# Decoding float64 weights on chip: the sign through a Prelu scaling, two bit operations in place of three, the weights of w2 in SBUF

## The chip, the cores and the metric

The kernel runs on one core of a Trainium2 chip. The metric is the device time of one execution in microseconds: 1180.98 us, the median of three runs (1179.63, 1183.80 and 1180.98 us). The engines of the core are TensorE (PE, matmuls, with its weight loads shown as PEld), VectorE (DVE), ScalarE (ACT), GpSimd (POOL) and SyncE (SP, which issues all DMAs here). Each works through its own instructions in order and waits on semaphores for the others.

## The reference

Three layers on 4608 tokens of width 512. Chunked attention: eight batches, eight heads, chunks of 64 tokens; then a SiLU layer of width 2048; then a layer of width 1024 with a softmax-weighted gate and a normalisation:

```
scores = scale * q_c @ k_c.T ; attn = softmax(scores) ; x = attn @ v_c
h = x @ w_in ;  x2 = (h * sigmoid(h)) @ w_out
h = x2 @ w_in2 ; solu = h * softmax(h)
ln = (solu - mean) / sqrt(var + 1e-6) * g_ln ;  out = ln @ w_out2
```

The four weight matrices arrive as float64 (w1 = w_in, w2 = w_out, w3 and w4 those of the last layer); q, k and v are float32.

## The kernel before

The tokens go through in nine blocks of 512. Every matrix product is made of three fp16 products: each operand is kept as a high and a low half (`split`, L107: the high half by ACT with a scale, the low half by a subtraction on DVE or POOL), and high x high, high x low and low x high are summed in PSUM. Blocks 0 and 1 multiply in this plain way (`h_group`, L357; `x_part`, L637). From block 2 on the layers use seven block products in place of eight (`h_fast`, `x_fast`, `m_fast`), whose weight sums are formed once, during blocks 1 and 2 (`w1_sums`, `w2_sums`, `w3_sums`), written to DRAM and streamed back through a ring of buffers.

A float64 weight has no engine type, so it is loaded as pairs of 32-bit words and decoded on chip, 128x512 values (a tile) at a time: 48 tiles, namely 16 of w1, 16 of w2 (index 16 to 31), 8 of w3 and 8 of w4. A tile goes through three steps, called in a software pipeline (`d1`, `d2`, `d3`, L869 to L887):

- `dec_scale` (L124): ACT reads the high word as if it were a float32 and multiplies it by a power of two, which moves the exponent into place.
- `dec_bits` (L131): DVE shifts the result left by three (L136), ORs in the top three bits of the low word (L137), and ORs in the sign bit, which the shift has lost, from the high word (L139). The scaled words p lie in PSUM for the tiles below `SB` = 32 (tile `wp`), from there on in SBUF (tile `wy`).
- `dec_split` (L142): the two halves, high on ACT (L110), low on POOL (L114), for w4 low on DVE (L115), with the factor g_ln folded in.

Where the decode calls stand among the other work is fixed by lists: `START` for the first 30 us or so (block 0's attention), `NW0` and `NX` during block 0, `NW1` and `NX1` during block 1; a scheduler then puts each engine's instructions in order, with the decode at a lower priority in places (`high_priority(offset=-50)`). The weight loads (`fetch`, L852) go through four SBUF buffers, and a tile's load is issued once an earlier tile's bits are done. `ytile` (L861) names the SBUF buffers for decoded tiles: five in turn up to tile 27, two from 28 on.

Attention of the next block runs inside the second layer of the present one (`step`, L977): scores, softmax, split of the softmax in a_norm (L229; the low half, L237, on POOL for block 0's calls, else on DVE), a DMA transpose (pT), and the product with v (a_pv, L256 to L258), which also needs v's halves vbh (ACT) and vbl (DVE). The second layer's chain of normalisation is `m_norm` (L740): row maximum (L670), exponential (L764), product (L766), and so on, while the scores h_ps stay in PSUM.

Of the kernel before, what the change touches and what calls it, by code (L numbers as in the profile page):

```python
# [40 lines left out]
S_LN = 2.0 ** 10  # L41

LEAST = -3.4028234663852886e38


@with_exitstack
def fused(ctx: ExitStack, tc: tile.TileContext, qkv, w1, w2, w3, w4, g_ln, out):
# [22 lines left out]
    QF = 14  # L70
    DEFER = 7

    const = ctx.enter_context(tc.tile_pool(name="const", bufs=1))
# [24 lines left out]
    mhalf = const.tile([P, 1], F32, name="mhalf")  # L98
    zero = const.tile([P, 1], F32, name="zero")


# [22 lines left out]
    def dec_scale(c):  # L124
        st, y, wh, wl, gain = c
        if c[1] is None:
            c[1] = ps1.tile([P, 512], I32, tag="mm", name="wp")
        p = c[1]
        A.activation(p.bitcast(F32), st[:, :, 1].bitcast(F32), AF.Copy, scale=2.0 ** -111)

    def dec_bits(c, y):  # L131
        st, p, wh, wl, gain = c
        c[1] = y
        if y is None:
            c[1] = y = p
        V.tensor_scalar(out=p, in0=p, scalar1=3, scalar2=None, op0=ALU.logical_shift_left)  # L136
        V.scalar_tensor_tensor(out=p, in0=st[:, :, 0], scalar=29, in1=p,  # L137
                               op0=ALU.logical_shift_right, op1=ALU.bitwise_or)
        V.scalar_tensor_tensor(out=y, in0=st[:, :, 1], scalar=-2 ** 31, in1=p,  # L139
                               op0=ALU.bitwise_and, op1=ALU.bitwise_or)  # L140

    def dec_split(c):  # L142
        st, y, wh, wl, gain = c
        yf = y.bitcast(F32)
        if len(wh.shape) == 3:
            yf = yf.rearrange("p (a b) -> p a b", a=wh.shape[1])
        if gain is None:
            split(wh, wl, yf, 1.0, A, G)
        else:
            split(wh, wl, yf, gain, A, V)  # L150

# [679 lines left out]
    G.memset(mhalf, -0.5)  # L831
    G.memset(zero, 0.0)
    ident = one.tile([P, P], F32, tag="h2", name="ident")
    make_identity(nc, ident)
# [24 lines left out]

    SB = 32  # L860
    def ytile(i):  # L861
# [22 lines left out]
    def d3():  # L884
        if out_:
            i, c = out_.pop(0)
            dec_split(c)  # L887

# [6 lines left out]
    for x in FIRST:  # L895
# [6 lines left out]
        else:  # L902
            t = len(vs0)
            vs0.append(one.tile([P, 512], F32, tag=("vs", "xb0", "xb1", "xb2")[t], name=f"vs0_{t}"))
            nc.sync.dma_start(out=vs0[t], in_=qkv[t, :, 2])
    nc.sync.dma_start(out=gs, in_=g_ln)


# [21 lines left out]
    for b in range(NB):  # L930
# [46 lines left out]
        def step(s):  # L977
# [13 lines left out]
            if s in AT_S:  # L991
# [3 lines left out]
                if i < 3:  # L995
                    prep_qk(m + ORDER[i + 1], V if b == 1 else G)
                a_norm(n, eng_l=V if b else G)
            if s in AT_P:
# [74 lines left out]
```

## Time and profile before

| | |
|---|---|
| median of three runs | 1180.98 us |
| the profiled execution, first to last instruction | 1179.4 us |
| TensorE busy | 1127.8 us, 96% |
| VectorE busy | 911.7 us, 77% |
| ScalarE busy | 802.8 us, 68% |
| GpSimd busy | 249.1 us, 21% |
| DMA, mean over the span | 177 GB/s |

The profile is of one execution, whose span of 1179.4 us lies close to the fastest of the runs. A busy share is an average over stages: the decode fills the first 190 us, and there the engines are used differently from the rest. In the rows below an instruction is named by its line, its engine, and the tile that it writes and reads (out<-in). A duration given for one instruction can overlap its neighbour's by a little, since an engine starts the next one before the last has drained. "Idle before" is the time in which the engine stood still ahead of such instructions, with what released it.

### The profile page before, as it was taken

The numbers are of one execution on the slowest core, as the hardware profiler recorded it, in microseconds if no ns is written. First come the engines' busy times: TensorE is split into PE (matmuls) and PEld (weight loads), VectorE is DVE, ScalarE is ACT, GpSimd is POOL, SyncE is SP. The second block draws the span as 40 slices with busy tenths as digits, with TensorE's granted clock in tenths as the row PEclk, the third lists the DMA queues.
The fourth block names the chain that finished last, engine by engine and source line by source line (L and its number), as shares of the span: only waits on it lengthen the run. The fifth ranks groups of instructions, "written<-read, shape, count | busy, mean of one in ns | idle before, by whom it ended". The sixth has DMA issues, their size and how long they took to land.

```text
span 1179.4 us, 23566 instructions
## 1 busy us (share of the span) xinstructions
PE 1127.8 (96%) x9036; PEld 769.1 (65%) x9036; DVE 911.7 (77%) x1638; ACT 802.8 (68%) x1475; POOL 249.1 (21%) x243
## 2 busy tenths in 40 slices
PE   5999998998999999999999999999999999999998
PEld 4444443444657875887678767876787677777853
DVE  5999998487578787888778877888689868886453
ACT  6886678676667777856785677568756876577253
POOL 3655433334101510021003100310031002100001
PEclk9999899999999999999999999999999999999999
DMA  7667488543536564776577657666776676665704
GB/s 259 225 190 206 155 233 268 165 135 112 139 113 203 165 189 133 204 204 202 143 192 213 196 151 188 204 198 155 182 211 198 161 180 197 179 161 137 210 21 116
DMA packets 205169, 209.18 MB, mean 177 GB/s; under 512 B 120192, under 2 KB 130432, under 8 KB 205056
## 3 DMA queue, kind: packets, MB, share of 16 engines
q1 hardware_dynamic: 205056, 207.68, 61.5%
q8 instruction: 70, 1.15, 0.4%
q14 instruction: 43, 0.35, 0.1%
HBM read 156.24 MB, written 24.12 MB: 153 GB/s over the span
## 4 chain that ended last, share of the span: by engine, by line
PE 59%; DVE 16%; ACT 10%; DMA 7%; issue 6%; POOL 2%; SPq 0%; ACTq 0%; POOLq 0%; DVEq 0%
PE o_ps L821 5%; PE o_ps L813 5%; PE o_ps L814 5%; PE pa L491 3%; PE pa L594 3%; PE pa L592 3%; PE pa L593 3%; PE pa L493 3%; PE pa L492 3%; DVE vbl L115 2%; PE pa L708 2%; PE pa L709 2%; PE pa L710 2%; PE pb L491 2%; PE pb L493 2%
## 5 line engine op out<-in xcount | busy, mean ns | idle before, releaser
L110 ACT ACTIVATE q<-hc 128x512 f16<-128x512 f32 x196 | 119.1, 624 | 41.4 <-DVE hc L579 16.4
L115 DVE SCALAR_TENSOR_TENSOR q<-hc,q 128x512 f16<-128x512 f32 x196 | 138.0, 719 | 6.9 <-ACT q L110 5.5
L114 POOL TENSOR_TENSOR qbl<-qk,qbh 64x512 f16<-64x512 f32 x54 | 71.0, 1314 | 266.2 <-ACT qbh L110 223.6
L593 PE MATMUL pa<-q,ring 128*128 128x256 f16 x448 | 122.1, 273 | 0.0
L592 PE MATMUL pa<-q,ring 128*128 128x256 f16 x448 | 122.1, 273 | 0.0
L594 PE MATMUL pa<-q,ring 128*128 128x256 f16 x448 | 122.1, 273 | 0.0
L813 PE MATMUL o_ps<-w4h,uT 128*128 128x512 f16 x288 | 109.1, 379 | 0.4 <-DVE e L766 0.4
L814 PE MATMUL o_ps<-w4l,uT 128*128 128x512 f16 x288 | 109.2, 379 | 0.0
L779 POOL TENSOR_TENSOR c<-c,mhalf 128x2 f32<-128x2 f32 (+1 forms) x22 | 14.1, 640 | 392.1 <-DVE c L778 382.2
L492 PEld LDWEIGHTS <-ring 128*128 128x128 f16 x784 | 77.0, 98 | 18.4 <-issue 7.9
L491 PEld LDWEIGHTS <-ring 128*128 128x128 f16 x784 | 77.0, 98 | 11.5 <-DMA ring<-w1s 0.8
L592 PEld LDWEIGHTS <-ring 128*128 128x128 f16 x784 | 76.7, 98 | 11.1
L593 PEld LDWEIGHTS <-ring 128*128 128x128 f16 x784 | 76.7, 98 | 11.0
L493 PEld LDWEIGHTS <-ring 128*128 128x128 f16 x784 | 77.0, 98 | 9.2
L594 PEld LDWEIGHTS <-ring 128*128 128x128 f16 x784 | 76.7, 98 | 8.9
L821 PE MATMUL o_ps<-w4h,uT 128*128 128x512 f16 x288 | 70.2, 379 | 0.0
L491 PE MATMUL pa<-x,ring 128*128 128x256 f16 x224 | 61.6, 275 | 6.7 <-ACT hc L513 4.3
L493 PE MATMUL pa<-x,ring 128*128 128x256 f16 x224 | 61.7, 275 | 0.0
L492 PE MATMUL pa<-x,ring 128*128 128x256 f16 x224 | 61.6, 275 | 0.0
L491 PE MATMUL pb<-x,ring 128*128 128x256 f16 x224 | 61.1, 273 | 0.6 <-DMA ring<-w1s 0.6
L592 PE MATMUL pb<-q,ring 128*128 128x256 f16 x224 | 61.1, 273 | 0.0
L593 PE MATMUL pb<-q,ring 128*128 128x256 f16 x224 | 61.1, 273 | 0.0
(277 smaller groups left out, 3486.4 us busy)
## 6 DMA issues: line engine op xcount, KB each, us to landing
ring<-w1s SPq DMA_DIRECT2D x196, 256.0 KB, 3.4
ring<-w2s SPq DMA_DIRECT2D x196, 256.0 KB, 3.8
wst<-w SPq DMA_DIRECT2D x48, 512.0 KB, 4.1
qk<-qkv SPq DMA_DIRECT2D x29, 512.0 KB, 3.8
vs<-qkv SPq DMA_DIRECT2D x36, 256.0 KB, 3.2
out<-o SPq DMA_DIRECT2D x36, 256.0 KB, 2.2
w1s<-ws SPq DMA_DIRECT2D x32, 128.0 KB, 2.1
w2s<-ws SPq DMA_DIRECT2D x16, 256.0 KB, 2.0
```

Of the source, the lines that this page charges most:

```text
L110: A.activation(dst_h, src, AF.Copy, scale=scale)
L114: return G.tensor_tensor(out=dst_l, in0=src, in1=dst_h, op=ALU.subtract).ins
L115: return V.scalar_tensor_tensor(out=dst_l, in0=src, scalar=scale, in1=dst_h, op0=ALU.mult, op1=ALU.subtract).ins
L491: T.matmul(ps[:, c], wh, x[:, 0, k], start=first, stop=False, skip_group_check=True)
L492: T.matmul(ps[:, c], wh, x[:, 1, k], start=False, stop=False, skip_group_check=True)
L493: T.matmul(ps[:, c], wl, x[:, 0, k], start=False, stop=k == 1, skip_group_check=True)
L592: T.matmul(ps[:, c], wh, g[:, 0], start=first, stop=False, skip_group_check=True)
L593: T.matmul(ps[:, c], wh, g[:, 1], start=False, stop=False, skip_group_check=True)
L594: T.matmul(ps[:, c], wl, g[:, 0], start=False, stop=q == 1 and f == 3, skip_group_check=True)
L813: T.matmul(ps, uh[:, k], w4h[:, k, :], start=k == 0, stop=False)
L814: T.matmul(ps, uh[:, k], w4l[:, k, :], start=False, stop=False)
L821: T.matmul(ps, ul[:, k], w4h[:, k, :], start=False, stop=k == K2 - 1)
```

## The change

The scaling becomes a Prelu with a scale of 2^-108 and a slope of -2^32 for negative input. A negative value comes out positive, with an exponent 32 higher; the shift by three then moves that 32 into the sign bit. So the sign is there after the shift, and the third bit operation falls away. All values are now too large by 2^24, and `dec_split` brings them back by `S_D` = 2^-24: for even tiles (V) the factor stands in both halves' operations, and the low half moves from POOL to DVE; for odd tiles of w1 (G) POOL multiplies the value in place by a constant tile `down` and subtracts; for odd tiles from w2 on (A) ACT scales the value in place, and POOL subtracts. For w4 the factor goes into gs, once, on POOL. `SB` goes from 32 to 16, so that w2's tiles lie in SBUF from the scaling on. The softmax's low half (L237) is on DVE in every block.

```diff
@@ constants
+S_D = 2.0 ** -24
+    WAYS = "VG" * 8 + "VA" * 12
+    down = const.tile([P, 1], F32, name="down")
@@ dec_scale
-        A.activation(p.bitcast(F32), st[:, :, 1].bitcast(F32), AF.Copy, scale=2.0 ** -111)
+        A.activation(p.bitcast(F32), st[:, :, 1].bitcast(F32), AF.Prelu, scale=2.0 ** -108, alpha=-2.0 ** 32)
@@ dec_bits
         V.tensor_scalar(out=p, in0=p, scalar1=3, scalar2=None, op0=ALU.logical_shift_left)
-        V.scalar_tensor_tensor(out=p, in0=st[:, :, 0], scalar=29, in1=p,
+        V.scalar_tensor_tensor(out=y, in0=st[:, :, 0], scalar=29, in1=p,
                                op0=ALU.logical_shift_right, op1=ALU.bitwise_or)
-        V.scalar_tensor_tensor(out=y, in0=st[:, :, 1], scalar=-2 ** 31, in1=p,
-                               op0=ALU.bitwise_and, op1=ALU.bitwise_or)
@@ dec_split
-        if gain is None:
-            split(wh, wl, yf, 1.0, A, G)
-        else:
-            split(wh, wl, yf, gain, A, V)
+        if gain is not None:
+            return split(wh, wl, yf, gain, A, V)
+        way = WAYS[i]
+        if way == "A":
+            A.activation(yf, yf, AF.Copy, scale=S_D)
+            return split(wh, wl, yf, 1.0, A, G)
+        if way == "G":
+            A.activation(wh, yf, AF.Copy, scale=S_D)
+            G.tensor_tensor(out=yf, in0=yf, in1=down.to_broadcast([P, 512]).rearrange("p (a b) -> p a b", a=KD)
+                            if len(yf.shape) == 3 else down.to_broadcast([P, 512]), op=ALU.mult)
+            return G.tensor_tensor(out=wl, in0=yf, in1=wh, op=ALU.subtract)
+        split(wh, wl, yf, S_D, A, V)
@@ further down
+    G.memset(down, S_D)
-    SB = 32
+    SB = 16
-            dec_split(c)
+            dec_split(c, i)
+    G.tensor_scalar(out=gs, in0=gs, scalar1=S_D, scalar2=None, op0=ALU.mult)
-                a_norm(n, eng_l=V if b else G)
+                a_norm(n)
```

The scheduler's order changes on DVE, ACT, POOL and SP; on PE it is the same. DVE has 1491 listed rows in place of 1519, POOL 137 in place of 140 and ACT 1125 in place of 1121. The listing numbers lines by each version's own file, so that the bits' L137 is L141 afterwards, and `split`'s low half L115 is L119.

First, DVE at the first normalisation of the last layer, during block 1; mp is the row maximum of the scores h_ps, e the product with the exponential. Before:

```order
L670 TENSOR_REDUCE mp<-h_ps 128x1 x2
L115 SCALAR_TENSOR_TENSOR w4l<-wy,gs,w4h 128x512
L672 TENSOR_REDUCE mm__1781<-mp 128x1
L137 SCALAR_TENSOR_TENSOR wy<-wst,wy 128x512
L761 TENSOR_SCALAR nm<-mm__1781 128x1
L136 TENSOR_SCALAR wy<-wy 128x512
L139 SCALAR_TENSOR_TENSOR wy<-wst,wy 128x512
L137 SCALAR_TENSOR_TENSOR wy<-wst,wy 128x512
L139 SCALAR_TENSOR_TENSOR wy<-wst,wy 128x512
L766 SCALAR_TENSOR_TENSOR e,us<-h_ps,u 128x512
```

The same place afterwards, with the last of the decode ahead of it:

```order
L141 SCALAR_TENSOR_TENSOR wy<-wst,wy 128x512
L119 SCALAR_TENSOR_TENSOR w4l<-wy,gs,w4h 128x512
L680 TENSOR_REDUCE mp<-h_ps 128x1 x2
L682 TENSOR_REDUCE mm__1745<-mp 128x1
L771 TENSOR_SCALAR nm<-mm__1745 128x1
L776 SCALAR_TENSOR_TENSOR e,us<-h_ps,u 128x512
```

The last tiles' bits stand ahead of the maximum now, not between it and the product.

Second, DVE in the first 30 us; am is the row maximum of a softmax of block 0, ae its exponentials, w_0 the first tile of w1. Before:

```order
L271 TENSOR_REDUCE am<-s_ps 128x8
L139 SCALAR_TENSOR_TENSOR wy<-wst,wp 128x512
L280 TENSOR_SCALAR am<-am 128x8
L286 TENSOR_SCALAR as<-as 128x8
L288 RECIPROCAL ar<-as 128x8
L271 TENSOR_REDUCE am<-s_ps 128x8
L290 TENSOR_TENSOR ae_225<-ae_225,ar 128x512
L280 TENSOR_SCALAR am<-am 128x8
L136 TENSOR_SCALAR wp<-wp 128x512
```

The same place afterwards:

```order
L281 TENSOR_REDUCE am<-s_ps 128x8
L119 SCALAR_TENSOR_TENSOR w_0_72<-wy,w_0_72 128x512
L290 TENSOR_SCALAR am<-am 128x8
L296 TENSOR_SCALAR as<-as 128x8
L298 RECIPROCAL ar<-as 128x8
L300 TENSOR_TENSOR ae_228<-ae_228,ar 128x512
L281 TENSOR_REDUCE am<-s_ps 128x8
L140 TENSOR_SCALAR wp<-wp 128x512
L290 TENSOR_SCALAR am<-am 128x8
```

The fourth softmax's maximum (the second am here) has moved behind the third's normalisation, and a shift stands between it and its scaling.

Third, POOL before, where it splits the first softmax for block 1 (ae), among the halves of q, k and w2:

```order
L114 TENSOR_TENSOR w2t<-wy,w2t 128x512 x3
L114 TENSOR_TENSOR qb<-qk,qb 64x8x64
L237 TENSOR_TENSOR ae<-ae 128x512
L114 TENSOR_TENSOR qb<-qk,qb 64x8x64
L114 TENSOR_TENSOR w2t<-wy,w2t 128x512 x2
```

And DVE afterwards, where that split stands now:

```order
L244 TENSOR_TENSOR ae<-ae,ar 128x512
L225 TENSOR_REDUCE am<-s_ps 128x8
L119 SCALAR_TENSOR_TENSOR w2t<-wy,w2t 128x512
L247 TENSOR_TENSOR ae<-ae 128x512
L230 TENSOR_SCALAR am<-am 128x8
```

The split (L237, now L247) left POOL's queue and stands on DVE, two rows behind the normalisation that it needs.

## Rows read from the trace of the kernel before

**Rows 1.** The page: busy us and share of each engine; granted clock in 40 slices.

```profile
PE 1127.8 (96%) x9036; PEld 769.1 (65%) x9036; DVE 911.7 (77%) x1638; ACT 802.8 (68%) x1475; POOL 249.1 (21%) x243
...
PEclk9999899999999999999999999999999999999999
```

**Rows 2.** Stretches: from:to, length, busy us of PE, PEld, DVE, ACT, POOL; PEclk, DMA.

```profile
30.00:70.00 40.00, 39.86 (x180) 17.78 (x179) 36.34 (x59) 34.63 (x63) 22.95 (x20) 0.96 0.65 217
70.00:120.00 50.00, 46.24 (x350) 23.07 (x348) 45.96 (x79) 37.15 (x89) 28.75 (x26) 0.97 0.67 200
120.00:150.00 30.00, 27.80 (x140) 13.21 (x141) 28.64 (x38) 21.29 (x36) 11.45 (x9) 0.89 0.49 144
150.00:200.00 50.00, 43.51 (x213) 20.70 (x212) 46.66 (x101) 40.25 (x74) 19.41 (x21) 1.00 0.88 263
320.00:1179.40 859.40, 844.30 (x7166) 621.26 (x7164) 659.46 (x1182) 571.58 (x981) 116.09 (x108) 1.00 0.62 173
90.00:100.00 10.00, 7.92 (x71) 4.05 (x70) 9.09 (x15) 6.89 (x13) 8.34 (x8) 0.83 0.84 220
120.00:130.00 10.00, 7.80 (x43) 3.78 (x44) 9.14 (x13) 6.63 (x12) 4.35 (x4) 0.66 0.57 184
```

**Rows 3.** PE's waits, 50 to 150, then 150 to 200: us, times, longest.

```profile
PE x_ps L256 <- ACT vbh L110: 2.1, 1, 2.1
PE x_ps L256 <- DMA pT<-ae: 2.1, 1, 2.1
PE x_ps L258 <- DVE vbl L115: 0.9, 2, 0.6
...
PE wq L391 <- DVE e L766: 2.9, 1, 2.9
PE h_ps L362 <- DVE y L406: 2.1, 1, 2.1
PE h_ps L362 <- ACT g L366: 0.8, 1, 0.8
```

**Rows 4.** DVE's groups, 20 to 200: xcount, busy us, mean ns, idle before.

```profile
L137 DVE SCALAR_TENSOR_TENSOR wp<-wst,wp 128x512 int32<-128x512 int32 x31 | 21.0, 687 | 0.2
L136 DVE TENSOR_SCALAR wp<-wp 128x512 int32<-128x512 int32 x31 | 21.0, 692 | 1.5 <-ACT wp L129 1.5
L139 DVE SCALAR_TENSOR_TENSOR wy<-wst,wp 128x512 int32<-128x512 int32 x31 | 20.8, 680 | 1.4 <-POOL w2t L114 1.0
L139 DVE SCALAR_TENSOR_TENSOR wy<-wst,wy 128x512 int32<-128x512 int32 x16 | 14.5, 904 | 0.3
L137 DVE SCALAR_TENSOR_TENSOR wy<-wst,wy 128x512 int32<-128x512 int32 x16 | 14.1, 878 | 0.3
L115 DVE SCALAR_TENSOR_TENSOR w4l<-wy,gs,w4h 128x512 f16<-128x512 f32 x8 | 7.4, 933 | 0.0
L136 DVE TENSOR_SCALAR wy<-wy 128x512 int32<-128x512 int32 x16 | 7.2, 449 | 0.4 <-ACT wy L129 0.4
```

**Rows 5.** Groups of ACT and POOL, 20 to 200 us, same columns.

```profile
L129 ACT ACTIVATE wy<-wst 128x512 f32<-128x512 f32 x16 | 10.8, 677 | 11.3 <-POOL w3q L114 6.7 <-DVE w4l L115 3.1 <-POOL w2t L114 1.4
...
L114 POOL TENSOR_TENSOR w2t<-wy,w2t 128x512 f16<-128x512 f32 x16 | 19.4, 1215 | 17.5 <-ACT w2t L110 12.1 <-DMA vs<-qkv 5.4
L237 POOL TENSOR_TENSOR ae<-ae 128x512 f16<-128x512 f32 x4 | 4.6, 1156 | 5.2 <-issue 5.2
```

**Rows 6.** Timeline of ACT at 28.9 us: start, us, instruction.

```profile
28.87 0.57 ACT L110 ACTIVATE x<-x_ps 128x512 f16<-128x512 f32 x1
```

**Rows 7.** Timeline of four instructions; in brackets the idle time before and its releaser.

```profile
86.16 0.61 ACT L236 ACTIVATE ae<-ae 128x512 f16<-128x512 f32 x1
...
88.04 1.15 POOL L237 TENSOR_TENSOR ae<-ae 128x512 f16<-128x512 f32 x1
...
118.57 0.69 DVE L139 SCALAR_TENSOR_TENSOR wy<-wst,wp 128x512 int32<-128x512 int32 x1 [1.05 <-POOL w2t L114]
...
119.29 0.63 ACT L110 ACTIVATE w2t<-wy 128x512 f16<-128x512 f32 x1 [2.46 <-DVE wy L139]
```

More of the change, by code (lines that the diff above doesn't have):

```diff
@@ L136, in dec_bits, with dec_split @@
         V.tensor_scalar(out=p, in0=p, scalar1=3, scalar2=None, op0=ALU.logical_shift_left)
-        V.scalar_tensor_tensor(out=p, in0=st[:, :, 0], scalar=29, in1=p,
+        V.scalar_tensor_tensor(out=y, in0=st[:, :, 0], scalar=29, in1=p,
                                op0=ALU.logical_shift_right, op1=ALU.bitwise_or)
-        V.scalar_tensor_tensor(out=y, in0=st[:, :, 1], scalar=-2 ** 31, in1=p,
-                               op0=ALU.bitwise_and, op1=ALU.bitwise_or)
-    def dec_split(c):
+    def dec_split(c, i):
         st, y, wh, wl, gain = c
```

## The prediction, made before the changed kernel ran

> **What bounds the kernel now.** I read the busy shares and the granted clock first [rows 1]: TensorE (PE) is busy 96% of 1179.4 us at a clock that is full in nearly every slice, so what is left to win is PE's idle time and its half-clock stretches. The stretches say where these are [rows 2]. From 320 us to the end PE is busy 844.30 of 859.4 us, and no weight is decoded there. From 70 to 200 us, the stretch of the decode that the change touches, PE loses 3.76 + 2.20 + 6.49 = 12.45 us, and the clock falls to 0.83 in 90 to 100 us and to 0.66 in 120 to 130 us: 10 x 0.17 = 1.7 us and 10 x 0.34 = 3.4 us of matmul time on top, each behind a wait of PE. VectorE (DVE) is busy 92 to 95% there, ScalarE (ACT) 71 to 81%, GpSimd (POOL) 38 to 58%. In 30 to 70 us DVE is nearly as full (91%), but PE stands still for 0.14 us only, so a faster decode buys nothing there.
>
> PE's waits [rows 3] name the two kinds of loss. In 50 to 150 us it waits 2.1 us for pT, the transposed softmax, 2.1 us for vbh and 0.9 us for vbl; in 150 to 200 us 2.9 + 2.1 us for e and y from DVE and 0.8 us for g from ACT. No wait is on a weight as such: PE waits for attention and normalisation steps that stand behind decode work on the in-order engines. Sum of these waits: 10.9 us; with the clock, 16.0 us. That is about the most a lighter decode can give back.
>
> **The change, part by part.** Durations are the means of [rows 4, 5].
>
> *w1, 16 tiles, bits still in PSUM.* Before 692 + 687 + 680 ns, after 692 + 687: 16 x 0.68 = 10.9 us less on DVE. Half of the tiles (V) now subtract on DVE: no row has this subtraction, it reads two SBUF operands. Between 0.69 (bits on PSUM) and 0.93 (w4l, the nearest form) I take 0.88, the bits on SBUF: 8 x 0.88 = 7.0. Net -3.9 us, beside a PE that doesn't wait in 30 to 70 us: nothing on the path.
>
> *w2, 16 tiles, bits moved to SBUF.* Before 16 x 2.06 = 32.9 us. After, shift 0.449 and or 0.878: 16 x 1.33 = 21.2, and 8 V subtractions 7.0: 28.3. Net -4.7 us.
>
> *w3, 8 tiles.* Before 8 x (0.449 + 0.878 + 0.904) = 17.8; after 8 x 1.33 + 4 x 0.88 = 14.1. Net -3.7 us.
>
> *w4, 8 tiles.* One operation of 0.904 less each: -7.2 us.
>
> *Block 1's attention split.* L237 goes from POOL (four of 1.156 us) to DVE: 4 x 0.88 = +3.5 us.
>
> DVE in sum: -3.9 - 4.7 - 3.7 - 7.2 + 3.5 = -16.0 us, of 157.6 us that it is busy in 30 to 200 us [rows 2]. POOL loses 40 subtractions and L237 and gains 8 multiplications and 20 subtractions, 16 x 1.2 = 19 us less. ACT gains 12 scalings of 0.68 (its SBUF to SBUF copy) = +8.1 us in 70 to 150 us, where it is busy 58.4 of 80 us: it becomes 83% full, still not the bound. Prelu has no row; I put it at the copy it replaces, bounded by 48 x 0.05 = 2.4 us either way (ACT's copies of this size differ by that: 0.677 in [rows 5], 0.63 in [rows 7]). The listing of ACT has 41 table loads before and after, so no load is added. The multiplication on POOL has no row either: POOL's subtraction, 1.2 us, bounded by half and double of it, on an engine half idle. The scaling of gs on POOL waits for a DMA of 4 KB issued at the start; ahead of POOL's first tile stand only fills, which it delays at no cost.
>
> The averages 878 and 904 against 687 and 680 on PSUM matter more than the operations. With PSUM as an operand, shift and or run undisturbed; with SBUF alone they are stretched by about 0.2 us on average, although POOL ran in both stretches. 28 operations of the w2 stage (16 ors, 8 subtractions, 4 L237) newly pay this; it is in the sum. The Trainium skill ("SBUF — State Buffer", section "SBUF: two separate sides") says why: VectorE with two SBUF inputs and a GpSimd operation share a port pair under an exclusive lock, and the loser waits for the whole instruction. It speaks against moving w2 to SBUF; what it would make of the time stands with the rivals. The trace agrees as to which operations suffer, but shows a mean of 0.2 us, not a whole 1.2 us.
>
> *The path.* Term by term against the 1179.4 us of this execution:
>
> Start. DVE's order puts the maximum of block 0's fourth softmax behind the third's normalisation (second order piece), some 0.69 us like every DVE operation of that size [rows 4]; ACT's exponentials wait for it, and ten operations of ACT, as many as before, stand between these and the last x, whose high part starts at 28.87 us [rows 6]. ACT isn't idle for all of it, and the first tile's low part now also sits on DVE. So the first matmul on x comes later by something between 0 and 1 us: I take +0.5 us.
>
> pT at 91 us [rows 7]. The last split of the softmax sits on POOL, where it starts at 88.04 us, 1.27 us after ACT's part ended (86.16 + 0.61), behind two others. On DVE (third order piece) this queue and 1.156 - 0.69 = 0.47 us go: the 2.1 us shrink by 1.7. Half of the clock's 1.7 us goes with it: together -2.6 us.
>
> vbh at 119 us [rows 7]. ACT stands 2.46 us at a w2 tile's high part, which waits for DVE's third bit operation, which waits 1.05 us for a buffer that POOL's subtraction of an earlier tile holds; vbh is queued behind. The third operation is gone, half of POOL's subtractions too. But the SBUF buffers are now held from the first step on, so a wait for a buffer moves to ACT's first step. I take half of 2.1 + 0.9 + 3.4 us: -3.2 us.
>
> 150 to 200 us. The first order piece shows DVE at the first softmax of the second layer: before, six decode operations stand between its maximum and its product, after, none: the bits of all 48 tiles are through. That takes 0.93 + 2 x 0.88 + 2 x 0.90 + 0.45 = 4.9 us out of this chain's queue, and something like it out of the next. Of the 5.8 us of waits I take two thirds: -3.8 us.
>
> 200 us on: the same work in the same order up to small shifts: 0, bounds -2 and +2 us (other transfers meet).
>
> Sum: +0.5 - 2.6 - 3.2 - 3.8 = -9.1, so 1170.3 us by the profile's span; the median of the runs lies 1.6 us above that span (1180.98 against 1179.4), which gives 1171.9 us. Own range of this case: 1167 to 1177.
>
> **The rivals.**
>
> *More comes back* (8%). All the waits of [rows 3] and both dips of the clock go: -16.0, less the start's +0.5: 1180.98 - 15.5 = 1165.5 us. For it: one late step feeds the next. Against: pT still takes its transpose, ACT is fuller.
>
> *The waits stay* (16%). DVE's relief is spent in idle time, since PE waits for chains that run over ACT, POOL and DMA in turn; ACT's +8.1 us fill the place. Only the 150 to 200 us term stays, halved, against the start: -1.9 + 0.5, about 1179.6 us. For it: DVE itself has gaps at 118.57 us because it waits for others.
>
> *The port takes more than the operations give: slower* (21%). In the w2 stage the bits alone would fall by 32.9 - 16 x 1.11 = 15.1 us (0.42 + 0.69 undisturbed), and 12 new operations cost 12 x 0.69 = 8.3: 6.8 us are won before any stretch. Shared over the 28 newly exposed operations this is 0.24 us each: above it the stage is slower on DVE than before, and 0.2 is what the trace shows now, with ACT fuller on top. If each of POOL's 14 operations left in that stage held DVE up for its whole 1.16 us, as the lock of the page would have it, DVE would spend 16.2 us, 9.4 us more than before; it has 4 us of room in 70 to 120 us [rows 2]. Then 5.4 us reach PE through pT and vbh, with the start's 0.5: 1180.98 + 5.9, about 1187 us. The last term of the sum is lost with it, since it needs the decode to be through in time.
>
> **How the numbers follow.** A measurement of this kernel tells 0.3% (3.5 us) from no change. Forecast 55%, more 8%, stay 16%, slower 21%. Faster by over 0.3% is below 1177.4: all but a few hundredths of the forecast and the whole of the first rival, 0.61. Within: the waits-stay case less its edges, and the edge of the forecast, 0.18. Slower: 0.21. The range reaches from 1163 (all comes back, with 2 us more from 200 us on) to 1185, which cuts off the worse part of the port rival.
>
> **What would show it.** Right: in 70 to 130 us no dip of the clock at 120 to 130; the ors on wy with a mean under 0.9 us; no PE wait on e or y above 1 us in 150 to 200; the first block of matmuls starting near 30.5 us; from 320 us on the same length as now. Wrong: a mean of the ors over 1.0 us, x_ps waiting longer for pT than 2.1 us, ACT waiting for a buffer of a w2 tile at its first step, or the whole gain or loss lying behind 320 us. If Prelu showed table loads or over 0.75 us, ACT would be the bound and the forecast fall with it.

## The result, and the profile after

The changed kernel takes 1192.94 us (median of four runs, 1191.90 to 1195.07) where the kernel before takes 1181.18 us beside it: ratio 1.0103, 95% interval [1.0087, 1.0120]. It is slower by 1%, and outside the predicted range, whose upper end was 1185.

The page after the change, as in [rows 1]:

```profile
PE 1128.7 (95%) x9036; PEld 769.5 (65%) x9036; DVE 895.2 (75%) x1614; ACT 808.7 (68%) x1487; POOL 233.1 (20%) x229
...
PEclk9997999999999999999999999999999999999999
```

VectorE does 16.5 us less, as reckoned (16.0), and TensorE's work is the same; yet the span grew by 10.7 us. The granted clock has its dip in the fourth slice now, 89 to 119 us, before in the fifth. Stretches after, in the columns of [rows 2], with one more slice:

```profile
30.00:70.00 40.00, 39.05 (x181) 17.66 (x181) 33.66 (x52) 33.20 (x60) 22.45 (x19) 1.00 0.66 217
70.00:120.00 50.00, 40.70 (x288) 20.33 (x287) 46.41 (x76) 43.09 (x100) 17.61 (x14) 0.86 0.66 193
120.00:150.00 30.00, 26.87 (x156) 12.27 (x155) 24.29 (x39) 22.93 (x39) 6.32 (x5) 0.94 0.68 201
150.00:200.00 50.00, 43.19 (x206) 20.38 (x205) 32.13 (x71) 36.50 (x67) 14.72 (x17) 0.97 0.77 229
90.00:100.00 10.00, 4.53 (x56) 2.92 (x55) 9.21 (x16) 7.52 (x27) 5.42 (x5) 0.72 0.58 161
120.00:130.00 10.00, 9.10 (x64) 4.33 (x62) 8.76 (x14) 7.69 (x14) 2.35 (x2) 1.00 0.55 157
100.00:110.00 10.00, 6.70 (x65) 3.73 (x64) 9.83 (x14) 8.20 (x15) 3.33 (x3) 0.84 0.88 257
```

The stretch that loses most is the one from 70 to 120 us: TensorE is busy there for 40.70 us, before for 46.24, and at a clock of 0.86 for 0.97. ScalarE, which the prediction took to have room, rose from 37.15 to 43.09 us there. Matching the matmuls of both traces one by one, since TensorE's order is the same, shows the loss in another way; the lag is the start of a matmul after the change minus its start before:

```
time before   33    80    91    94   103   107   120   130   140   160   190   220   310  1170 us
lag         -0.2  -1.2  -0.5  +3.2  +7.0  +9.4  +7.5  +4.8  +8.9  +8.9 +12.7  +9.7 +10.7 +10.7 us
```

Ten microseconds are lost between 91 and 107 us, in the attention of block 1. By 130 us 4.6 of them are back, at the place where the kernel before has its own wait for vbh and its half clock; by 140 us 4.1 are lost again, where the first matmuls of block 1's first layer wait for x and the clock falls (0.66 from 138 to 143 us, before 1.00). So the loss is made in two places. TensorE's waits from 50 to 150 us, as the first part of [rows 3]:

```profile
PE x_ps L266 <- DMA pT<-ae: 5.5, 1, 5.5
PE x_ps L266 <- ACT vbh L114: 2.5, 2, 2.2
PE x_ps L268 <- DVE vbl L119: 1.9, 2, 1.1
PE h_ps L372 <- ACT x L114: 1.1, 1, 1.1
PE h_ps L373 <- DVE x L119: 0.9, 1, 0.9
```

And from 150 to 200 us, as its second part:

```profile
PE h_ps L674 <- DVE y L416: 4.1, 2, 2.1
PE h_ps L372 <- DVE e L776: 1.6, 1, 1.6
```

The wait for pT is 5.5 us in place of 2.1. VectorE's operations themselves, groups from 20 to 200 us as in [rows 4]:

```profile
L141 DVE SCALAR_TENSOR_TENSOR wy<-wst,wy 128x512 int32<-128x512 int32 x32 | 22.9, 723 | 0.6
L140 DVE TENSOR_SCALAR wy<-wy 128x512 int32<-128x512 int32 x32 | 16.9, 532 | 7.6 <-ACT wy L133 7.6
...
L119 DVE SCALAR_TENSOR_TENSOR w2t<-wy,w2t 128x512 f16<-128x512 f32 x8 | 6.4, 804 | 0.0
```

The or is shorter than reckoned (723 ns on average for 878) and the shift longer (532 for 449); together they take 1.26 us a tile, where 1.33 were expected, and the subtraction 0.80 for 0.88. But VectorE stood still 7.6 us in front of shifts whose words ScalarE hadn't scaled. ScalarE's groups, as in [rows 5], say why:

```profile
L133 ACT ACTIVATE wy<-wst 128x512 f32<-128x512 f32 x32 | 21.2, 677 | 10.4 <-DMA wst<-w 5.2 <-POOL w3q L118 4.0 <-DVE w4l L119 0.8
...
L133 ACT ACTIVATE wp<-wst 128x512 f32<-128x512 f32 x14 | 8.7, 631 | 0.0
L153 ACT ACTIVATE wy<-wy 128x512 f32<-128x512 f32 x12 | 7.6, 634 | 2.8 <-DVE wy L141 2.7
```

Prelu costs what the copy cost (677 ns into SBUF, 631 into PSUM). But ScalarE waits 5.2 us for loads of weights (wst) at the scaling, and while it waits, all that stands behind the scaling in its queue waits too. The timeline of ScalarE after the change; L376 is a SiLU of block 0's first layer, of which there are 16, L235 the exponential of block 1's first softmax, whose table load comes first:

```profile
60.95 0.68 ACT L133 ACTIVATE wy<-wst 128x512 f32<-128x512 f32 x1 [2.09 <-DMA wst<-w]
61.52 0.64 ACT L133 ACTIVATE wp<-wst 128x512 f32<-128x512 f32 x1
62.08 0.57 ACT L376 ACTIVATE h_ps<-h_ps 128x512 f32<-128x512 f32 x1
62.56 0.64 ACT L133 ACTIVATE wp<-wst 128x512 f32<-128x512 f32 x1
...
68.78 0.67 ACT L133 ACTIVATE wy<-wst 128x512 f32<-128x512 f32 x1 [1.51 <-DMA wst<-w]
...
81.50 0.62 ACT L376 ACTIVATE h_ps<-h_ps 128x512 f32<-128x512 f32 x1
...
85.56 1.28 ACT L235 ACT_TABLE_LOAD   x1
```

The same place before:

```profile
58.15 0.62 ACT L129 ACTIVATE wp<-wst 128x512 f32<-128x512 f32 x1
58.71 0.55 ACT L366 ACTIVATE h_ps<-h_ps 128x512 f32<-128x512 f32 x1
...
59.95 0.62 ACT L129 ACTIVATE wp<-wst 128x512 f32<-128x512 f32 x1
...
61.57 0.64 ACT L129 ACTIVATE wp<-wst 128x512 f32<-128x512 f32 x1 [1.00 <-DMA wst<-w]
...
75.95 0.55 ACT L366 ACTIVATE h_ps<-h_ps 128x512 f32<-128x512 f32 x1
...
79.97 1.28 ACT L225 ACT_TABLE_LOAD   x1
```

Before, the last two tiles of w1 are scaled at 58.15 and 59.95 us, the tenth SiLU between them, and the first tile of w2 behind them, at 61.57. After, the first tile of w2 (wy) stands ahead of both (wp) and of the SiLU, and its load lands late: ScalarE waits 2.09 us, from 58.86 on, with a SiLU behind it whose input must be there: TensorE is 0.2 us ahead of the kernel before, which started that SiLU at 58.71. The tenth SiLU starts 3.4 us later, the last one 5.6 us later, and the exponential with it. The chain goes from there over the normalisation and the split to pT's transpose (issued at 89.2 us before, 93.3 after) and ends in TensorE's wait for pT. The normalisation before, then the normalisation and the two halves of the split after:

```profile
84.99 0.68 DVE L234 TENSOR_TENSOR ae<-ae,ar 128x512 f32<-128x512 f32 x1
...
90.79 0.68 DVE L244 TENSOR_TENSOR ae<-ae,ar 128x512 f32<-128x512 f32 x1
...
91.51 0.63 ACT L246 ACTIVATE ae<-ae 128x512 f16<-128x512 f32 x1 [1.35 <-DVE ae L244]
...
92.59 0.68 DVE L247 TENSOR_TENSOR ae<-ae 128x512 f16<-128x512 f32 x1
```

All this is an observation; whether it is the cause the runs had to tell.

### The profile page after: what moved, and what is told of

The parts are those of the page before. It is cut to its first block, busy times and chain, and to the rows that moved or that the text cites. A ratio compares the mean times of both kernels' runs of the same rounds, so it can differ in the third digit from the quotient of the medians.

```text
span 1190.1 us, 23534 instructions
## 1 busy us (share of the span) xinstructions
PE 1128.7 (95%) x9036; PEld 769.5 (65%) x9036; DVE 895.2 (75%) x1614; ACT 808.7 (68%) x1487; POOL 233.1 (20%) x229
## 4 chain that ended last, share of the span: by engine, by line
PE 56%; DVE 17%; ACT 11%; DMA 5%; issue 5%; POOL 2%; POOLq 0%; SPq 0%; ACTq 0%; DVEq 0%
PE o_ps L823 4%; PE o_ps L824 4%; PE o_ps L831 4%; PE pa L604 3%; PE pa L603 3%; PE pa L602 3%; PE pa L501 3%; PE pa L503 3%; PE pa L502 3%; DVE vbl L119 2%; PE pa L720 2%; PE pa L719 2%; PE pa L718 2%; DMA wst<-w 2%; ACT u L782 2%
## 5 line engine op out<-in xcount | busy, mean ns | idle before, releaser
L119 DVE SCALAR_TENSOR_TENSOR q<-hc,q 128x512 f16<-128x512 f32 x196 | 137.7, 718 | 7.0 <-ACT q L114 5.5
L501 PE MATMUL pa<-x,ring 128*128 128x256 f16 x224 | 61.0, 272 | 8.4 <-ACT hc L523 5.3
L501 PE MATMUL pa<-xb,ring 128*128 128x256 f16 x224 | 61.1, 273 | 0.0
L502 PE MATMUL pa<-xb,ring 128*128 128x256 f16 x224 | 61.1, 273 | 0.0
L602 PE MATMUL pb<-q,ring 128*128 128x256 f16 x224 | 61.1, 273 | 0.0
L503 PE MATMUL pa<-xb,ring 128*128 128x256 f16 x224 | 61.1, 273 | 0.0
```

The costliest lines, as they stand in the source:

```text
L119: return V.scalar_tensor_tensor(out=dst_l, in0=src, scalar=scale, in1=dst_h, op0=ALU.mult, op1=ALU.subtract).ins
L501: T.matmul(ps[:, c], wh, x[:, 0, k], start=first, stop=False, skip_group_check=True)
L502: T.matmul(ps[:, c], wh, x[:, 1, k], start=False, stop=False, skip_group_check=True)
L503: T.matmul(ps[:, c], wl, x[:, 0, k], start=False, stop=k == 1, skip_group_check=True)
L602: T.matmul(ps[:, c], wh, g[:, 0], start=first, stop=False, skip_group_check=True)
```

## The experiments

All ratios are to the kernel before, on the same chip at the same time, with 95% intervals.

**First theories: VectorE's queue, or the place of w2's bits.** In the changed kernel the bits of 24 tiles stand ahead of block 1's first softmax maximum on VectorE, 20 before. Four runs; `maxes[m]` is that maximum.

```diff
@@ e1_max_first: the changed kernel; e4_sb16_max_first: the kernel before, with SB = 16 too
...
-                with tc.high_priority(offset=-50):
+                with tc.high_priority(offset=-50), tc.issue_after(maxes[m]):
                     weights(NX[s])
@@ e2_before_late: the kernel before, four decode calls moved ahead of the first scores
-    NX = [2, 3, 2, 1, 0, 6, 0, 2]
+    NX = [0, 1, 2, 1, 0, 6, 0, 2]
...
+            if b == 0 and s == 0:
+                weights(4)
@@ e3_after_sb32: the changed kernel
-    SB = 16
+    SB = 32
```

> The changed kernel, with the decode calls of block 0's second layer queued, on VectorE, behind the row maximum of block 1's first softmax: 20 tiles' bits stand ahead of that maximum, as in the kernel before, where the changed kernel has 24. Nothing else is changed. Theory A (the order): the maximum was late by 6.8 us (83.23 against 76.40 us) because four tiles that wait for their loads stood ahead of it, and PE's 5.6 us wait for pT with the half clock behind it follows from that. Then the 7 us lost between 91 and 110 us come back: about 1185 us, PE's first wait for pT under 2.5 us. Rival B (the port): two-operand operations on SBUF are held up by POOL and the w2 stage is slower whatever the order: within 3 us of the changed kernel's 1192.9. Rival C (ACT, fuller by Prelu and 12 scalings): also within 3 us of 1192.9.

Measured: 1191.56, ratio 1.0093 [1.0065, 1.0121]. The theory fails: the maximum was queued first and still started at 82.2 us. ScalarE's splits of g, which VectorE needs ahead of it, stood behind scalings that waited for loads (1.88 us at 77.0).

> The kernel before, with four of the decode calls of block 0's second layer traced ahead of block 1's first scores (and taken out of the list behind), so that 24 tiles' bits stand ahead of the first maximum. Three bit operations, w2 in PSUM, no Prelu. Theory A: the kernel before becomes slower by this order alone, by at least half of what the change cost: 1187 to 1193 us, with a first wait for pT of 5 us or more. Rivals B and C: the order alone costs little, 1181 to 1184 us.

Measured: 1183.31, ratio 1.0026 [1.0013, 1.0039]. Decode ahead of the attention costs something, but some 3 us, not 12. This run tells more than that: its first maximum starts at 85.1 us and its first wait for pT is 4.7 us, nearly as in the changed kernel, and yet most of it is given back behind. A late pT alone doesn't make the loss of the changed kernel.

> The changed kernel with w2's bits in PSUM again (SB = 32); Prelu, two bit operations and the three ways of splitting stay. 21 tiles' bits then stand ahead of the first maximum. Theory A: without the late order the loss up to 110 us is gone: 1180 to 1186 us. Rival B (port): also fast again, since PSUM operands are not held up, so this run doesn't tell A from B. Rival C (ACT): stays at 1190 to 1193 us.

Measured: 1182.46, ratio 1.0016 [1.0003, 1.0029]. With w2's bits back in PSUM 10 of the 12 us are gone; Prelu, the two operations and the new splits together cost about 2 us. The rival that ScalarE is simply fuller falls with it, since this run has all of ScalarE's new operations.

> The kernel before with w2's bits moved to SBUF (SB = 16), all else as it was, and the maximum kept in its place (20 tiles ahead) by the same queueing as in e1. It has three bit operations on SBUF per w2 tile. Theory A: without the late order the move to SBUF is cheap: 1178 to 1184 us. Rival B (port): 32 or more two-operand operations on SBUF are held up by POOL, which here still does all 16 subtractions of w2: 1186 us or more.

Measured: 1198.35, ratio 1.0154 [1.0134, 1.0174]. The move to SBUF, with the maximum kept first, slows the kernel before by more than the change does. So SB = 16 is the edit that costs. It does three things: it puts both operands of the bits in SBUF, beside GpSimd; it holds a tile's buffer from the scaling on; and it lets the scheduler choose another order.

**Which of the three.** The runs with SB = 16 and with SB = 32 issue the same instructions in the same program order, so one can be held to the other's queue order:

```diff
+    order = {'DVE': [...], 'Activation': [...], 'Pool': [...]}
+    traced = {i.name: i for i in nc.cur_bb.bb.instructions}
+    for row in order.values():
+        for p, n in zip(row, row[1:]):
+            tc.add_manual_dep(traced[f"I-{n}"], f"I-{p}", mybir.DependencyInfo(
+                mybir.DependencyClass.NoSync, mybir.DependencyReason.DATA), reason="order")
```

The edges are meant to set an order of issue and add no wait; engines that aren't held get the scheduler's order, which can come out otherwise beside a held one. Two runs needed both buffers held, by one-element operations:

```diff
@@ e11_psum_held (SB = 32), in d1 and d2
+            if 16 <= i < SB:
+                held[i] = ytile(i)
+                A.activation(held[i].bitcast(F32)[:, 0:1], st[:, 0:1, 1].bitcast(F32), AF.Copy)
...
+            if i in held:
+                z = sml.tile([P, 1], F32, tag="hold", name="held")
+                V.tensor_copy(out=z, in_=held[i].bitcast(F32)[:, 0:1])
...
@@ e12_sbuf_pinned (SB = 16): the same on a PSUM bank, and the order of e11_psum_held
```

> The changed kernel with w2's bits back in PSUM (as in the run with SB=32, 1182.5 us), but each w2 tile's SBUF buffer is taken already at its scaling, as it is in the changed kernel, by one element that ScalarE writes, and read by one element on VectorE at its bit operations; so it holds the buffers of both kernels. Theory B (buffers held from the scaling on make the loss): about 1190. Theory O (the order in which VectorE and ScalarE get the decode makes it; 21 tiles' bits stand ahead of block 1's first maximum here, as with SB=32): 1181 to 1184. Theory L (operations on two SBUF operands lose to GpSimd at a shared port): 1181 to 1184, since the bits stay in PSUM.

> As the run before, with one thing changed: w2's scaled values and bits lie in the SBUF buffer, as in the changed kernel; the PSUM bank is taken all the same, by one element, and VectorE, ScalarE and GpSimd are held to the order of the run before up to w2's last tiles. Same order, same buffers, only the place of the values differs. Theory O and theory B: within 2 us of the run before. Theory L: 6 to 10 us above it, with w2's bit operations longer by 0.1 us and more and pT at 90 us late again.

> The changed kernel, nothing in it but the order changed: VectorE, ScalarE and GpSimd are held to the order of the run with bits in PSUM and buffers held, up to w2's last tiles. Theory O: 1181 to 1185, most of the 12 us back. Theory L: about 1190, since every operation still works on two SBUF operands. Theory B: about 1190, since the buffers are held as in the changed kernel.

Measured: 1186.92 (1.0055 [1.0036, 1.0075]), 1190.82 (1.0089 [1.0073, 1.0105]) and 1181.67 (1.0010 [0.9999, 1.0020]). The third decides: the changed kernel with nothing but the order changed loses its loss, although its bits still lie in SBUF and its buffers are still held from the scaling on. Theory O holds. The first pair tells little: the second run of it has the order and the place of the bits in common with the third, and lies 9 us above it, with nothing more than the 32 small operations (0.16 to 0.20 us each on ScalarE) and the PSUM banks that they hold. Beside that, the 3.9 us between the two can't be put down to the place of the bits.

**Which engine's order.**

> The changed kernel with ScalarE alone held to the order that brought it to 1181.7 us; VectorE's order is the scheduler's. Theory O-S (ScalarE's queue is what holds the attention up: scalings that wait for a load stand ahead of the splits and exponentials): 1181 to 1184. Theory O-V (VectorE's queue does: decode ahead of the maxima): about 1188 to 1191, unless VectorE's order follows.

> The changed kernel with VectorE alone held to that order; ScalarE's is the scheduler's. Theory O-V: 1181 to 1184. Theory O-S: 1187 to 1191, with the splits and exponentials on ScalarE late, and VectorE's first maximum of block 1 late for it, at 80 us and after, as in the run that moved the first maximum alone.

Measured: ScalarE alone 1182.26 (1.0017 [1.0004, 1.0031]); VectorE alone 1192.11 (1.0094 [1.0068, 1.0121]). It is ScalarE's queue that has to be held. VectorE's order was free in the first of the two runs, but it didn't stay that of the changed kernel: the bits of 21 tiles stand ahead of block 1's first maximum there, in place of 24. In the second run it is 21 as well, and the loss stays: VectorE's order without ScalarE's gives nothing back. The timeline of ScalarE with its order held, to be laid beside the two above:

```profile
59.88 0.63 ACT L133 ACTIVATE wp<-wst 128x512 f32<-128x512 f32 x1
60.45 0.56 ACT L376 ACTIVATE h_ps<-h_ps 128x512 f32<-128x512 f32 x1
60.92 0.63 ACT L133 ACTIVATE wp<-wst 128x512 f32<-128x512 f32 x1
...
62.14 0.67 ACT L133 ACTIVATE wy<-wst 128x512 f32<-128x512 f32 x1 [0.59 <-DMA wst<-w]
...
76.37 0.58 ACT L376 ACTIVATE h_ps<-h_ps 128x512 f32<-128x512 f32 x1
...
80.39 1.28 ACT L235 ACT_TABLE_LOAD   x1
```

The tiles are scaled in their order again, w2's first waits 0.59 us, and the last SiLU is back at 76.4 us. The lag by matmuls, as for the changed kernel above, in the profiled executions of this run (its slowest, 1184.9 us) and of three others (e19_no_pool is explained below):

```
time before        33    91    94   107   130   140   160   190   310  1170 us
changed          -0.2  -0.5  +3.2  +9.4  +4.8  +8.9  +8.9 +12.7 +10.7 +10.7
e14_pin_scalar   +0.9  -0.1  -2.1  +6.8  +0.8  +0.8  +2.0  +1.2  +2.5  +3.7
e13_after_pinned -0.3  -1.3  -3.2  +3.6  -2.0  -0.9  -0.9  -0.5  -0.4  -0.2
e19_no_pool       0.0  -1.0  -1.1  +0.8  -4.4  -3.4  -3.4  -5.1  -4.9  -2.2
e2_before_late   -0.1  +1.2  +4.1  +7.2  +1.2  +2.6  +2.6  +3.5  +2.9  +1.3
```

With ScalarE's order held the wait for pT is gone, and the 4.1 us between 130 and 140 us are gone too: of the 8.1 us between the two runs at 140 us, half comes there. The loss between 94 and 107 us stays: 6.2 us in the changed kernel, 8.9 with ScalarE alone held, 6.8 with all three engines; there TensorE waits for vbh and vbl, in e13_after_pinned:

```profile
PE x_ps L266 <- ACT vbh L114: 4.2, 1, 4.2
PE x_ps L268 <- DVE vbl L119: 1.5, 1, 1.5
```

ScalarE's queue, counted in the traces; in the upper rows stand the two kernels and runs of the changed one that differ from it in order or in SB alone, in the lower ones runs that don't fit:

```
                   tenth SiLU   scalings ahead    last SiLU   ScalarE idle at
                   starts at    of the last SiLU  starts at   scalings, 60 to 85   time
before               58.7            22             76.0           2.5            1181.2
changed              62.1            24             81.5           4.6            1192.9
e1_max_first         62.4            24             82.0           6.1            1191.6
e15_pin_vector       63.2            23             81.4           5.4            1192.1
e14_pin_scalar       60.4            21             76.4           0.6            1182.3
e13_after_pinned     59.2            21             76.2           0.1            1181.7
e3_after_sb32        59.3            21             76.3           1.3            1182.5
e16_as_before        59.8            22             77.5           2.0            1183.4

e2_before_late       58.6            22             75.7           6.4            1183.3
e12_sbuf_pinned      59.2            21             77.7           0.0            1190.8
e4_sb16_max_first    58.4            23             79.2           3.1            1198.4
e20_before_sb16_pinned 58.6          22             75.4           2.4            1194.0
```

In the upper rows a last SiLU after 81 us goes with 1191 us and more, one before 78 us with 1184 and less. Between the changed kernel and e14_pin_scalar, three scalings more stand ahead of the last SiLU (1.9 us of work), ScalarE stands still 4.0 us longer at scalings whose loads haven't landed, and the last SiLU is 5.1 us later. The lower rows are slow or fast for something else: e2_before_late has the idle time and not the late SiLU, and the other three have earlier SiLUs than the changed kernel and yet take 1190 us and more.

**With the order of before, what are the operations worth?** The prediction reckoned with an unchanged order around the attention and came to 1170.

> The changed kernel with VectorE, ScalarE and GpSimd held to the order of the kernel before as far as w2's last tiles (its new operations, which that order doesn't have, stand where their inputs allow). It takes the order out of the comparison: what is left is the operations. If the prediction's terms were right for an unchanged order: 1170 to 1175. If VectorE's saved time is hidden there or eaten by the new operations on ScalarE: 1179 to 1183. If the port matters: 1185 and above.

> The same with w2's bits in PSUM (SB=32), in the order of the kernel before. It keeps the Prelu, the two bit operations and the splits of the change and drops only the move to SBUF. Its order differs from the run with SB=32 alone (1182.5) by little: 1178 to 1182. If the place of w2's bits matters by itself, in equal order, it and the run before it lie apart by over 3 us.

> The kernel before, where only w4's 8 tiles use the Prelu scaling and two bit operations, with 2^-24 put into the gain; w1, w2 and w3 are decoded as before. It removes 8 VectorE operations of about 0.88 us and adds nothing. If VectorE's work between 150 and 200 us is worth anything as the prediction had it: 1176 to 1179. If it is hidden: 1180, no difference. If even this reorders the attention: 1183 and above.

Measured: 1183.39 (1.0016 [1.0002, 1.0030]), 1182.61 (1.0016 [1.0004, 1.0028]), and for w4 alone 1179.64 (0.9992 [0.9979, 1.0005]). Between the first two only SB differs, and they come out alike: in this order it makes no difference that can be measured whether w2's bits lie in SBUF or in PSUM. And the 16 us on VectorE are worth nothing in the order of before, set against what the change adds on ScalarE; eight operations less in w4, about 7 us of VectorE, nothing that can be told from no change.

**Where VectorE's saved time goes.** In the run with the good order the shift of a w2 tile took 0.42 us while GpSimd stood still and up to 1.38 while it worked. Two rows of e13_after_pinned, two shifts in the first, of which the one that starts after GpSimd's operation takes 1.38:

```profile
88.56 1.72 DVE L140 TENSOR_SCALAR wy<-wy 128x512 int32<-128x512 int32 x2
88.59 1.40 POOL L118 TENSOR_TENSOR qb<-qk,qb 64x512 f16<-64x512 f32 x1 [3.50 <-ACT qb L114]
```

```diff
@@ e19_no_pool (in the order of e13_after_pinned) and e6_no_pool_free_order (in the scheduler's)
-    WAYS = "VG" * 8 + "VA" * 12
+    WAYS = "VG" * 8 + "V" * 16 + "VA" * 4
@@ e24_scale_kept, in the order of e13_after_pinned; way B for w2's odd tiles
-    WAYS = "VG" * 8 + "VA" * 12
+    WAYS = "VG" * 8 + "VB" * 8 + "VA" * 4
...
-        if way == "A":
+        if way in "AB":
             A.activation(yf, yf, AF.Copy, scale=S_D)
-            return split(wh, wl, yf, 1.0, A, G)
+            return split(wh, wl, yf, 1.0, A, G if way == "A" else V)
@@ e21_values_early: two pairs of vbh and vbl moved forward in the order of e13_after_pinned; e22_both: with e19's edit
```

> The changed kernel in the order that brought it to 1181.7 us, with all 16 tiles of w2 split as its way V does: ScalarE and VectorE scale and split, GpSimd has nothing to do for w2 and ScalarE's extra scalings of w2 go (6 on ScalarE and 6 on GpSimd less, 6 of about 0.7 us on VectorE more). In that run's trace VectorE's shift took 1.38 us beside a GpSimd subtraction and 0.42 without one, about 5 us in all between 80 and 100 us. If those waits at the shared port cost the gain: 1176 to 1179. If they are hidden: 1181 to 1183.

> The changed kernel in the order that brought it to 1181.7 us, with one thing moved: the splits of the values (vbh on ScalarE, vbl on VectorE) of block 1's second and third attention tile stand right behind the split of the tile before them, not behind three to five instructions of the weights' decode. In that run TensorE waits 4.2 us for vbh at 99 us and 1.5 us for vbl, while ScalarE stood 2.4 us at a scaling that waited for VectorE's bits, with the splits behind it. If ScalarE's queue also hides what VectorE saves: 1175 to 1178, faster than both kernels. If the transposed probabilities (pT, started at 97.6) are hardly earlier than vbh: 1180 to 1182.

> Both edits of the two runs before it that concern the change: no GpSimd for w2, and the values' splits early. If both are worth something: 1172 to 1177. If the first is hidden: as the run with the values early.

Measured: 1176.66 (0.9968 [0.9957, 0.9979]), 1182.78 (1.0028 [1.0012, 1.0043]) and 1176.10 (0.9963 [0.9949, 0.9977]). (Eight odd tiles of w2 move from GpSimd, where the expectation counted six.) Without GpSimd and without ScalarE's extra scalings in w2 the change is a gain at last, and the kernel beats both. The lag table shows where: between 94 and 107 us this kernel loses 1.9 us in place of 6.8. The early values are a miss, alone and on top (the third can't be told from the first): the wait for vbh went, and TensorE waited for pT and w2 in its place:

```profile
PE x_ps L266 <- DMA pT<-ae: 3.7, 1, 3.7
PE x_ps L655 <- ACT w2t L114: 3.4, 2, 2.2
```

> The run without GpSimd in w2 (1176.7 us) took away two things at once: GpSimd's subtractions and ScalarE's extra scalings of the odd tiles. Here, in the same order, the odd tiles of w2 keep ScalarE's scaling, and only the subtraction moves from GpSimd to VectorE. If GpSimd beside VectorE was the cost: 1176 to 1178. If ScalarE's scalings (0.63 us each) were: 1181 to 1183.

Measured: 1178.59 (0.9987 [0.9976, 0.9999]), between the two. By the ratios, GpSimd's subtractions are worth some 0.23% (2.7 us) and ScalarE's scalings some 0.19% (2.2 us); with intervals of 0.1% on each side, that split is rough. VectorE's shifts and ors from 70 to 120 us, in e13_after_pinned:

```profile
L141 DVE SCALAR_TENSOR_TENSOR wy<-wst,wy 128x512 int32<-128x512 int32 x14 | 11.5, 824 | 0.1
L140 DVE TENSOR_SCALAR wy<-wy 128x512 int32<-128x512 int32 x14 | 8.8, 637 | 4.5 <-ACT wy L133 4.5
```

and in e24_scale_kept:

```profile
L141 DVE SCALAR_TENSOR_TENSOR wy<-wst,wy 128x512 int32<-128x512 int32 x14 | 11.4, 823 | 0.1
L140 DVE TENSOR_SCALAR wy<-wy 128x512 int32<-128x512 int32 x14 | 6.8, 488 | 0.2 <-ACT wy L133 0.2
```

The shifts lose 2.0 us, the wait for ScalarE ahead of them 4.3. GpSimd still works on q and k there: the two ors over 1 us in this stretch (1.65 and 1.64) lie beside such operations, and the mean of the ors is as it was.

> The changed kernel with all 16 tiles of w2 split as way V (no GpSimd, no extra scaling for w2), and every engine in the scheduler's own order. It completes the square of order and GpSimd: own order with GpSimd 1192.9 us, ScalarE's better order with GpSimd 1181.7, the better order without GpSimd 1176.7. If the two are separate: about 1187 to 1188. If without GpSimd the scheduler finds a good order by itself: 1176 to 1180.

Measured: 1188.82 (1.0065 [1.0048, 1.0081]). The two causes add up within the intervals: by the ratios the split of w2 is worth 0.38% in the scheduler's order and 0.42% in the held one (4.5 and 5 us), the order, held on three engines, 0.93% with GpSimd and 0.97% without (11 us).

> The kernel before with w2's bits in SBUF (SB=16) and the first maximum kept first, which took 1198.4 us, with ScalarE alone held to the order of the kernel before. Theory O-S (ScalarE's order makes the loss, and the place of the bits only through it): 1181 to 1186. If the place of the bits costs by itself in the kernel before (three bit operations on two SBUF operands, GpSimd beside them): 1192 and above.

Measured: 1194.04 (1.0120 [1.0105, 1.0135]). This one went against the theory. In the kernel before, with three operations per tile and GpSimd taking every subtraction, ScalarE's order is not what makes the loss. Its groups from 70 to 120 us, to be read against 0.69 us on PSUM in [rows 4]:

```profile
L137 DVE SCALAR_TENSOR_TENSOR wy<-wst,wy 128x512 int32<-128x512 int32 x12 | 11.9, 1004 | 0.2
L139 DVE SCALAR_TENSOR_TENSOR wy<-wst,wy 128x512 int32<-128x512 int32 x12 | 11.2, 950 | 0.1
L136 DVE TENSOR_SCALAR wy<-wy 128x512 int32<-128x512 int32 x12 | 10.3, 866 | 1.8 <-ACT wy L129 1.8
```

That is 2.82 us for a tile where PSUM takes 2.06, 9 us in all for these twelve. VectorE's and GpSimd's order weren't held here, and the buffers are held longer, so that the place alone makes the loss of 14 us isn't shown. In the changed kernel, with two operations and fewer of GpSimd's, what GpSimd costs is a matter of 3 us.

What stays open: why the scheduler sends ScalarE's scalings ahead when the bits lie in SBUF. That such a scaling needs no PSUM bank, and so finds its buffer free earlier, is argued only; the order was taken as given and replaced. No run has the kernel before in the changed kernel's order. Why the small operations of the two runs with held buffers cost as much as they do, and how the loss of the kernel before with its bits in SBUF divides, isn't settled either.

## Why the prediction was wrong, point by point

*VectorE's sum: right.* -16.0 predicted, -16.5 measured over the whole span, with one reading wrong in it: the shift was counted as undisturbed in SBUF (0.449), and it was stretched too (0.532, and 0.63 from 70 to 120 us). ScalarE's +8.1 from 70 to 150 us came out as +7.6 there (58.44 to 66.02), GpSimd's -19 as -16.0. Prelu at the price of the copy was right (677 and 631 ns), with 41 table loads as before.

*The start: hidden.* +0.5 predicted, between 0 and 1; the first matmul on x starts 0.9 us later (30.43 for 29.49). That it costs nothing is luck: the granted clock from 30 to 33 us is 1.00, before 0.52, and from 33 us on the matmuls are 0.2 us early.

*pT at 91 us: the step that failed.* Predicted -2.6; the wait grew by 3.4 us, and the lag by 10 within 16 us, with the clock (0.72 from 90 to 100 us, 0.83 before) and the waits for vbh and vbl that follow. The prediction said that "this queue and 1.156 - 0.69 = 0.47 us go", and most of it did go: the low half starts 1.1 us after the high one (91.51 and 92.59), before 1.9, and takes 0.68 us. But it took the rest of the chain as fixed. The normalisation ahead of it came 5.8 us later, because ScalarE's queue held the SiLUs, the splits of g and the exponential behind scalings that waited for loads. The order had been read on VectorE and GpSimd, on ScalarE only for the start; behind that ScalarE was reckoned by its busy time ("83% full, still not the bound"). Full or not, it was late. With ScalarE's order held the normalisation is back at 85.4 us, and the lag falls by 2.0 us at this place: for an unchanged order the term was about right. What the prediction lacked even then is a term for the second attention tile: 6.8 us from 94 to 107 us, at vbh and vbl, which in e13_after_pinned eat what pT and the wait at 119 us give. In e19_no_pool, which loses 1.9 us there, the time falls to 1176.7.

*vbh at 119 us: right there, lost elsewhere.* The wait at 119 us is gone, and the clock from 120 to 130 us rose from 0.66 to 1.00; predicted -3.2, the lag falls by 4.6 us from 107 to 130 us. But 4.1 us are lost again by 140 us, and vbh and vbl still cost 2.5 + 1.9 us, at other places. The clock in this sum was no firm ground either: in e8_w4_only, which decodes w1, w2 and w3 as before, it is 1.00 from 90 to 100 and from 120 to 130 us, and the time is the same. The sentence that "a wait for a buffer moves to ACT's first step" named the right engine and step; what it waits for from 60 to 86 us is a load (4.6 us), a buffer only later (4.0 us for w3q).

*150 to 200 us: wrong.* Predicted -3.8. VectorE's busy time in this stretch fell from 46.66 to 32.13 us, and TensorE's idle time rose from 6.49 to 6.81. The decode left the chain from the maximum to the product, and the wait for e fell from 2.9 us to 1.6; but the one for y rose from 2.1 to 4.1. Why isn't shown. w4's operations alone, taken away in the kernel before, give nothing.

*From 200 us on: right.* The lag stays between 9.3 and 11.5 us.

*The rivals.* "Slower" was the side that came, at 21%, but its mechanism decides only a part. With all of GpSimd's operations left in, holding ScalarE's order brings the time back to 1182.3. GpSimd's subtractions beside VectorE are worth about 3 us in the changed kernel; a mean of the ors over 1.0 us, named as its sign, was not seen (0.72). Single rows are longer: in the changed kernel one or of 0.69 us took 1.65, beside a GpSimd subtraction of 1.49 that had started 0.39 us earlier. The rival's rule, the lock of the page "SBUF — State Buffer", section "SBUF: two separate sides", in the Trainium skill, has the later one wait for the whole instruction of the other; such rows agree with it better than the mean from before the change had suggested. "The waits stay" (1179.6) comes nearest to what the change is worth in the order of before, 1182 to 1183.

## What to carry to other kernels

Before an engine's saved time is counted, read the order of every engine that feeds the chain on the path, also of one with room: scalings whose loads hadn't landed, a few places further ahead in ScalarE's in-order queue, cost some 11 us here, and 16 us less on VectorE gave nothing that could be measured in the old order. Where two versions issue the same instructions, holding one to the other's order, engine by engine, separates order from operations, as long as one looks at what the free engines did. Operations added to hold a buffer weren't a neutral tool. The order held on three engines and w2 split by ScalarE and VectorE alone made together of a loss of 1.0% a gain of 0.3%.

## What the runs showed of the hardware

A shift on VectorE with source and target in SBUF takes 0.42 us alone and up to 1.38 beside a GpSimd operation of 1.4 us; from PSUM to PSUM it takes 0.69 either way. The or takes 0.68 to 0.69 us from either place while GpSimd is quiet; beside GpSimd it took up to 1.66 us with both operands in SBUF and at most 0.69 with one in PSUM (e13_after_pinned). So SBUF is the faster place for the shift only as long as GpSimd is quiet, and for the or it gained nothing. Prelu with a scale and a slope costs ScalarE what a scaled copy costs (631 ns into PSUM, 677 into SBUF), and loads no table of its own.
